# Attention with mixed heads and a gated MLP on one core: the sign of the converted weights set as a bit on VectorE instead of multiplied in on GpSimd

## The chip, the cores and the metric

The kernel runs on one core of one Trainium2 chip, as one program. The metric is its time on the device in microseconds, from the first to the last instruction with what lies around it; lower is better. A core has five engines with a queue each, which run side by side and wait for each other by semaphores: TensorE (PE in the profile, PEld its weight loads), VectorE (DVE), ScalarE (ACT), GpSimd (POOL) and SyncE (SP). Here SP does no arithmetic, it issues nearly all the DMAs. An engine takes its instructions strictly in order: one that waits holds up everything behind it in the same queue. All tensors lie in SBUF while they are worked on; matmuls write to PSUM.

## The reference

```python
# attention: 4 batches, 12 heads, 448 positions, head size 64 (q, k, v, w_pre, w_post)
scores = scale * np.matmul(q, k.transpose(0, 1, 3, 2))
scores = np.einsum('bhij,hg->bgij', scores, w_pre)
scores = scores - np.max(scores, axis=-1, keepdims=True)
attn = np.exp(scores)
attn = attn / (np.sum(attn, axis=-1, keepdims=True) + 1e-09)
attn = np.einsum('bhij,hg->bgij', attn, w_post)
attn_out = np.matmul(attn, v)
x = attn_out.transpose(0, 2, 1, 3).reshape(1792, 768)
# gated MLP, d_model 768, d_ff 1536
g = x @ w_gate
silu = g * (1.0 / (1.0 + np.exp(-g)))
out = (silu * (x @ w_val)) @ w_out
```

The three weight matrices of the MLP come as 64-bit floats. [...]

## The kernel before

The attention runs first, over four batches with 45 row blocks each (reshuffle by DMA, split into a high and a low part, three pre matmuls, max, exp, post matmuls, and per head the product with v); its result goes to HBM as x in a high and a low part. Behind it the MLP runs over two halves of the tokens (first and second batch of 896). For each it goes over 12 blocks f of d_ff: `up` computes g and v for two halves of 448 tokens, with a weight tile of 768 columns per block for each of g and v (a unit; unit 2f is g's, unit 2f + 1 is v's), and three matmuls per product (high times high, low times high, high times low). `gate`, `gated` and `gated_low` make of them the tiles sg, m, gh and gl. Then come three thirds of the output with 4 units each (`down`, `finish`).

In the first half each of the 36 units is loaded as raw 64-bit words (`load_raw`, issued by SP, line 437), converted (`convert`), stored as 32-bit floats for the second half (`keep`, SP, line 475) and split (`split_w`: whi on ACT at line 492, wlo on DVE at line 488). In the second half it is only loaded again (`load_w`) and split. Of raw and mag there are two buffers each, so unit n + 2 can be loaded only when every reader of raw of unit n is done; of w there are three, of whi and wlo four.

`convert` has nine steps, and each is a single instruction. ACT takes the high word, read as a 32-bit float, and makes its magnitude (Abs, line 456) and its sign (Sign, line 458, values 1 and -1). The magnitude is clamped (line 460). DVE works on the integer words: it moves the exponent (462), takes the exponent alone into w (464), shifts the magnitude into place (466), multiplies the low word by it (468) and adds the two (470). The last step multiplies w by the sign (472). `eng`, which clamps and multiplies, is POOL, and DVE for the first three units (EARLY), which are converted while the attention still runs.

The order of the work is written out by numbers: every step is put down with a due time by `at` or, for the MLP, `at_ff`, and `run` sorts by it and issues in that order; the queue of an engine is the sorted list cut to that engine. In the MLP a step of `convert` is due some 16 to 6 units of time ahead of the matmuls that need the weights. There x in `at_ff(n - x, ...)` is read from a list of nine numbers, one per step. Around it the queue of DVE goes round in a fixed turn for each f, two units per turn: m and gl of the two halves lie between the steps of the one unit, and the steps of the other stand together; wlo of a unit stands behind the add (470) of the unit after it.

Of the kernel before, what the change touches and what calls it, by code (L numbers as in the profile page):

```python
# [11 lines left out]
F32 = mybir.dt.float32  # L12
F32R = mybir.dt.float32r
U32 = mybir.dt.uint32
AF = mybir.ActivationFunctionType
ALU = mybir.AluOpType
# [3 lines left out]
def f32_of(bits):  # L20
    return struct.unpack("<f", struct.pack("<I", bits))[0]
# [3 lines left out]
def talking_heads_moe_kernel(ctx, tc, q, k, v, w_pre, w_post, w_gate, w_val, w_out, out):  # L25
    nc = tc.nc
# [3 lines left out]
    P = 128  # L30
# [42 lines left out]
    def at(key, fn):  # L73
        ops.append((key, len(ops), fn))
# [7 lines left out]
    def later(fn, *a):  # L82
        return lambda: fn(*a)
# [43 lines left out]
    def first(c):  # L127
        return c * QT
# [222 lines left out]
    for b in range(B):  # L351
# [3 lines left out]
        for p in range(NPAIR):  # L355
            n = n0 - 22 + 1.9 * p if b else (-30.5 + 0.5 * p if p < 2 else -30.5 + p)
# [3 lines left out]
        for c in range(NC):  # L360

            n = n0 + first(c)
            if (b, c) == (0, 0):
                load, ready, step = -61, -31, 1.0
                score = -29.0
            else:
                before = tiles((c - 1) % NC)
                step = before / NPAIR
# [12 lines left out]
        for t in range(NTB):  # L381
            n = n0 + t
# [12 lines left out]
        for c0, m in parts:  # L395
            last = n0 - (-(c0 + m) * CP // TS) - 1
            for p in range(NPAIR):
                n = last + (5 + p * 1.45 if m == 2 else 4.9 + AVS * p if c0 + m == NC else 5 + AVO + AVS * p)
# [6 lines left out]
    pl = {}  # L405
# [6 lines left out]
    W = NKC * P  # L412
    EARLY = 3
    raws, cvs, w32, wsp, xs_, ups, sgs, ms, g_, yps = ({} for _ in range(10))
# [14 lines left out]
    def unit_index(u):  # L429
        if u[0] == "o":  # L430
            return 2 * NFC + u[1] * (NFC * ET // W) + u[2]
        return 2 * u[1] + (u[0] == "v")
# [9 lines left out]
    def convert(u, step):  # L442
        n = unit_index(u)
        eng = nc.vector if n < EARLY else nc.gpsimd
        if step == 0:
            mag, sgn, w = (
                pl["cv_p"].tile([P, W], F32, tag=x, name=f"{x}_{n}", bufs=k) for x, k in (("mag", 2), ("sgn", 2), ("w", 3))
            )
            cvs[u] = mag, sgn
            w32[0, u] = w  # L450
        mag, sgn = cvs[u]
        w = w32[0, u]
        low, high = raws[u][:, :, 0], raws[u].bitcast(F32)[:, :, 1]
        a, b = mag.bitcast(U32), w.bitcast(U32)
        if step == 0:
            nc.scalar.activation(mag, high, AF.Abs)  # L456
        elif step == 1:
            nc.scalar.activation(sgn, high, AF.Sign)
        elif step == 2:
            eng.tensor_scalar(mag, mag, f32_of(0x38000000), f32_of(0x47EFFFFF), op0=ALU.max, op1=ALU.min)  # L460
        elif step == 3:
            nc.vector.tensor_scalar(a, a, 0x08000000, 4, op0=ALU.bitwise_xor, op1=ALU.logical_shift_left)  # L462
        elif step == 4:
            nc.vector.tensor_scalar(b, a, 1, 0x7F800000, op0=ALU.logical_shift_right, op1=ALU.bitwise_and)
        elif step == 5:
            nc.vector.tensor_scalar(a, a, 1, None, op0=ALU.logical_shift_right)
        elif step == 6:
            nc.vector.scalar_tensor_tensor(w, low, 2.0 ** -52, w, op0=ALU.mult, op1=ALU.mult)
        elif step == 7:
            nc.vector.tensor_tensor(w, mag, w, op=ALU.add)  # L470
        else:
            eng.tensor_tensor(w, w, sgn, op=ALU.mult)  # L472

    def keep(u):
        nc.sync.dma_start(out=w_d[unit_index(u)], in_=w32[0, u])
# [94 lines left out]
    def at_ff(n, fn):  # L570
        at(END + n / 1.8, fn)

    for b in range(NT // TB):
# [7 lines left out]
        for f in range(NFC):  # L581
            n = n0 + f * T_F
# [11 lines left out]
        for e in range(3):  # L594
# [4 lines left out]
            if last:  # L599
                for c in range(NTC):  # L600
                    n = n1 + c * NFC * T_D / NTC
# [10 lines left out]
        for n, u in units:  # L612
            if b:
                at_ff(n - 16, later(load_w, b, u))
                at_ff(n - 8, later(split_w, b, u, False))
                at_ff(n - 7, later(split_w, b, u, True))
            elif unit_index(u) < EARLY:
                n = START + SPACE * unit_index(u)
                at(max(START, n - 4.0), later(load_raw, u))
                for step, x in enumerate((0.4, 0.8, 0.5, 0.5, 1.8, 2.5, 2.9, 4.1, 5.1)):  # L620
                    at(n + x + 0.25, later(convert, u, step))
                at(n + 8.4, later(split_w, b, u, False))
                at(n + 10.6, later(split_w, b, u, True))
                at(n + 6.7, later(keep, u))
            else:
                n -= LEAD
                n1 = END + (n - 21.3) / 1.8
                at(min(n1, B * NTB + 2.75) if unit_index(u) == EARLY else n1, later(load_raw, u))
                for step, x in enumerate((16.2, 15, 15.4, 12.6, 12.1, 11.6, 11.1, 10.2, 5.8)):
                    at_ff(n - x, later(convert, u, step))  # L630
                at_ff(n - 3.8, later(split_w, b, u, False))
                at_ff(n - 2.8, later(split_w, b, u, True))
                at_ff(n - 3.9, later(keep, u))
# [43 lines left out]
```

## Time and profile before

| | |
|---|---|
| median of 3 runs (1045.07 to 1048.63) | 1047.21 us |
| the profiled execution | 1048.95 us |
| its span, from first to last instruction | 1047.2 us |
| PE busy | 1020.7 us, 97% |
| PEld busy | 853.2 us, 81% |
| DVE busy | 597.8 us, 57% |
| ACT busy | 514.1 us, 49% |
| POOL busy | 444.0 us, 42% |
| mean granted clock of TensorE | 0.995 |

A share of the span is an average over stages that differ: the attention up to about 500 us, the first half of the MLP up to about 778 us with the conversion in it, then the second half without it. A busy PE is one that has a matmul under way, not one at its peak. A wait is put down to the one that came last. Times of rows are counted from the start of the span. In the names of tiles a number of the buffer is left out: `mag<-raw` is any unit's.

### The profile page before, as it was taken

To read this page: it belongs to the slowest core of one execution; us is meant where nothing else is said; L and a number is where in the kernel's file an instruction comes from. 1 tells how busy PE (TensorE), PEld (TensorE's weight loads), DVE (VectorE), ACT (ScalarE), POOL (GpSimd) and SP (SyncE) were. 2 spreads that over 40 slices of the span, in tenths; PEclk is the share of its full clock that TensorE was granted. 3 is DMA by queue.
4 is the path that set the end of the run, shared out by engine and by line. 5 is a ranking of instruction groups with operands and counts; after the bars stand their busy time and mean duration, and the time that the engine had idled before them with its cause. 6 is when DMAs were issued, how large, how long until landed. Compare 5 with 4: busy or idle time off the path is not lost.

```text
span 1047.2 us, 17964 instructions
## 1 busy us (share of the span) xinstructions
PE 1020.7 (97%) x6660; PEld 853.2 (81%) x6660; DVE 597.8 (57%) x1181; ACT 514.1 (49%) x1103; POOL 444.0 (42%) x439
## 2 busy tenths in 40 slices
PE   6899999999999999999999999999999999999998
PEld 3577777777777777777898888899999999999998
DVE  4566555657466565577499999998923322332110
ACT  2686776768676676786444434443322222222110
POOL 1675555647465555674375666667600000000000
PEclk9999999999999999998999999999999999999999
DMA  6466443844466443668554444448741112112311
GB/s 125 117 160 172 116 126 112 202 132 125 124 160 176 116 127 113 183 199 244 183 166 151 147 169 138 160 155 289 254 167 46 60 47 61 46 61 62 97 50 36
DMA packets 131055, 140.69 MB, mean 134 GB/s; under 512 B 52552, under 2 KB 114012, under 8 KB 130968
## 3 DMA queue, kind: packets, MB, share of 16 engines
q1 hardware_dynamic: 130776, 139.30, 45.3%
q8 instruction: 53, 0.87, 0.4%
q0 software_dynamic: 192, 0.24, 0.1%
q14 instruction: 34, 0.28, 0.1%
HBM read 70.19 MB, written 30.80 MB: 96 GB/s over the span
## 4 chain that ended last, share of the span: by engine, by line
PE 76%; DVE 13%; ACT 3%; issue 3%; DMA 3%; POOL 2%; SPq 0%; POOLq 0%; ACTq 0%; DVEq 0%
PE post L306 14%; PE qk L224 8%; PE av L328 7%; PE dn L547 5%; PE dn L546 5%; PE dn L548 5%; PE pre L271 5%; PE pre L273 3%; PE pre L272 3%; DVE w L470 3%; DVE mag L462 3%; PE upv L508 3%; PE upv L507 3%; PE upg L512 3%; PE upg L508 3%; PE upg L507 3%
## 5 line engine op out<-in xcount | busy, mean ns | idle before, releaser
L265 POOL TENSOR_TENSOR lo<-rs,hi 120x448 fp32r<-120x448 f32 x180 | 206.5, 1148 | 161.0 <-ACT hi L259 157.6
L306 PEld LDWEIGHTS post<-rw,e 120*112 120x112 f32 (+1 forms) x1440 | 169.9, 177 | 32.2 <-issue 9.6
L306 PE MATMUL post<-rw,e 120*112 120x120 f32 (+1 forms) x1440 | 181.7, 270 | 0.3 <-POOL rw L296 0.3
L460 POOL TENSOR_SCALAR mag<-mag 128x768 f32<-128x768 f32 x33 | 103.8, 3145 | 95.9 <-ACT mag L456 94.1
L547 PE MATMUL dn<-wlo,gh 128*128 128x256 f32 x504 | 141.1, 280 | 0.5 <-DVE wlo L488 0.5
L546 PE MATMUL dn<-whi,gh 128*128 128x256 f32 x504 | 141.0, 280 | 0.0
L548 PE MATMUL dn<-whi,gl 128*128 128x256 f32 x504 | 141.0, 280 | 0.0
L280 DVE TENSOR_REDUCE st<-pre 120x1 f32<-120x448 f32 x180 | 111.8, 621 | 39.8 <-PE pre L273 36.9
L315 ACT ACTIVATE attnT<-post 112x480 f32<-112x480 f32 (+3 forms) x192 | 103.5, 546 | 28.4 <-PE post L306 26.3
L287 ACT ACTIVATE e<-pre,st 120x448 f32<-120x448 f32 x180 | 114.0, 633 | 0.5 <-DVE st L280 0.5
L259 ACT ACTIVATE hi<-rs 120x448 fp32r<-120x448 f32 x180 | 103.9, 577 | 17.7 <-DMA rs<-stg 9.6
L508 PE MATMUL upv<-x,wlo 128*128 128x448 f32 x288 | 106.5, 370 | 4.7 <-DVE wlo L488 4.7
L488 DVE TENSOR_TENSOR wlo<-w,whi 128x768 fp32r<-128x768 f32 x72 | 69.1, 961 | 72.2 <-ACT whi L492 70.8
L230 DVE COPY stg<-qk 110x448 f32<-110x448 f32 (+1 forms) x144 | 85.1, 619 | 43.1 <-PE qk L224 42.5
L507 PE MATMUL upg<-x,whi 128*128 128x448 f32 x288 | 105.8, 367 | 0.0
L508 PE MATMUL upg<-x,wlo 128*128 128x448 f32 x288 | 105.6, 367 | 0.0
L507 PE MATMUL upv<-x,whi 128*128 128x448 f32 x288 | 105.6, 367 | 0.0
L224 PE MATMUL qk<-kk,qt 64*110 64x448 f32 (+1 forms) x384 | 100.3, 594 | 4.4 <-DVE stg L230 2.8
L492 ACT ACTIVATE whi<-w 128x768 fp32r<-128x768 f32 x72 | 60.2, 839 | 87.8 <-POOL w L472 57.9
L528 ACT ACTIVATE gh<-m 128x448 fp32r<-128x448 f32 x48 | 27.8, 579 | 137.8 <-DVE m L523 137.8
L547 PEld LDWEIGHTS dn<-wlo,gh 128*128 128x128 f32 x504 | 94.7, 188 | 0.7 <-DVE wlo L488 0.7
L546 PEld LDWEIGHTS dn<-whi,gh 128*128 128x128 f32 x504 | 94.7, 188 | 0.0
(65 smaller groups left out, 1786.7 us busy)
## 6 DMA issues: line engine op xcount, KB each, us to landing
rs<-stg SPq DMA_DIRECT2D x176, 210.0 KB
w_d<-w SPq DMA_DIRECT2D x36, 384.0 KB
w<-w_d SPq DMA_DIRECT2D x36, 384.0 KB
x<-x_d SPq DMA_DIRECT2D x24, 448.0 KB
x_d<-xs SPq DMA_DIRECT2D x42, 224.0 KB
raw<-in_moe_w_gate_dram SPq DMA_DIRECT2D x12, 768.0 KB
raw<-in_moe_w_val_dram SPq DMA_DIRECT2D x12, 768.0 KB
raw<-in_moe_w_out_dram SPq DMA_DIRECT2D x12, 768.0 KB
```

Source lines behind the costliest of these rows:

```text
L224: nc.tensor.matmul(pt[:m], qt[b, c][hs, p, :m], kk[b, p][hs], start=True, stop=True)
L259: nc.scalar.activation(hi[:n], x[:n], AF.Copy)
L265: nc.gpsimd.tensor_tensor(lo[:n], x[:n], hi[:n].bitcast(F32), op=ALU.subtract)
L280: nc.vector.tensor_reduce(st[:n, 0:1], pt[:n], axis=AX.X, op=ALU.max, negate=True)
L287: nc.scalar.activation(e[:n], pt[:n], AF.Exp, bias=st[:n, 0:1], scale=1.0, accum_out=st[:n, 1:2])
L306: nc.tensor.matmul(pt[:, c, :, :m], e[:n, c * CP:(c + 1) * CP], w[:n, :, :m], start=True, stop=True)
L460: eng.tensor_scalar(mag, mag, f32_of(0x38000000), f32_of(0x47EFFFFF), op0=ALU.max, op1=ALU.min)
L507: nc.tensor.matmul(pt, hi[:, c], xh[:, c, ts], start=(c == 0), stop=False)
L508: nc.tensor.matmul(pt, lo[:, c], xh[:, c, ts], start=False, stop=False)
L546: nc.tensor.matmul(pt, gh, hi, start=opens, stop=False)
L547: nc.tensor.matmul(pt, gh, lo, start=False, stop=False)
L548: nc.tensor.matmul(pt, gl, hi, start=False, stop=closes)
```

## The change

Step 1, Sign on ACT, goes, and with it the tile sgn. The other steps move up by one number. The last step is no longer a float product of w and sgn on POOL (on DVE for the first three units) but one scalar_tensor_tensor on DVE for all 36 units: of the high word of raw all bits but the sign bit are masked out, and the result is or-ed into w, both read as 32-bit integers. So raw has a reader at the end of the conversion, and the store of w and whi wait for DVE instead of POOL. In the MLP the due time of the last step goes from 5.8 to 9.3 ahead of the unit.

```diff
@@ -443,33 +443,31 @@
         n = unit_index(u)
         eng = nc.vector if n < EARLY else nc.gpsimd
         if step == 0:
-            mag, sgn, w = (
-                pl["cv_p"].tile([P, W], F32, tag=x, name=f"{x}_{n}", bufs=k) for x, k in (("mag", 2), ("sgn", 2), ("w", 3))
+            mag, w = (
+                pl["cv_p"].tile([P, W], F32, tag=x, name=f"{x}_{n}", bufs=k) for x, k in (("mag", 2), ("w", 3))
             )
-            cvs[u] = mag, sgn
+            cvs[u] = mag
             w32[0, u] = w
-        mag, sgn = cvs[u]
+        mag = cvs[u]
         w = w32[0, u]
         low, high = raws[u][:, :, 0], raws[u].bitcast(F32)[:, :, 1]
         a, b = mag.bitcast(U32), w.bitcast(U32)
         if step == 0:
             nc.scalar.activation(mag, high, AF.Abs)
         elif step == 1:
-            nc.scalar.activation(sgn, high, AF.Sign)
+            eng.tensor_scalar(mag, mag, f32_of(0x38000000), f32_of(0x47EFFFFF), op0=ALU.max, op1=ALU.min)
         elif step == 2:
-            eng.tensor_scalar(mag, mag, f32_of(0x38000000), f32_of(0x47EFFFFF), op0=ALU.max, op1=ALU.min)
+            nc.vector.tensor_scalar(a, a, 0x08000000, 4, op0=ALU.bitwise_xor, op1=ALU.logical_shift_left)
         elif step == 3:
-            nc.vector.tensor_scalar(a, a, 0x08000000, 4, op0=ALU.bitwise_xor, op1=ALU.logical_shift_left)
+            nc.vector.tensor_scalar(b, a, 1, 0x7F800000, op0=ALU.logical_shift_right, op1=ALU.bitwise_and)
         elif step == 4:
-            nc.vector.tensor_scalar(b, a, 1, 0x7F800000, op0=ALU.logical_shift_right, op1=ALU.bitwise_and)
+            nc.vector.tensor_scalar(a, a, 1, None, op0=ALU.logical_shift_right)
         elif step == 5:
-            nc.vector.tensor_scalar(a, a, 1, None, op0=ALU.logical_shift_right)
+            nc.vector.scalar_tensor_tensor(w, low, 2.0 ** -52, w, op0=ALU.mult, op1=ALU.mult)
         elif step == 6:
-            nc.vector.scalar_tensor_tensor(w, low, 2.0 ** -52, w, op0=ALU.mult, op1=ALU.mult)
-        elif step == 7:
             nc.vector.tensor_tensor(w, mag, w, op=ALU.add)
         else:
-            eng.tensor_tensor(w, w, sgn, op=ALU.mult)
+            nc.vector.scalar_tensor_tensor(b, raws[u][:, :, 1], 0x80000000, b, op0=ALU.bitwise_and, op1=ALU.bitwise_or)
 
     def keep(u):
         nc.sync.dma_start(out=w_d[unit_index(u)], in_=w32[0, u])
@@ -617,7 +615,7 @@
             elif unit_index(u) < EARLY:
                 n = START + SPACE * unit_index(u)
                 at(max(START, n - 4.0), later(load_raw, u))
-                for step, x in enumerate((0.4, 0.8, 0.5, 0.5, 1.8, 2.5, 2.9, 4.1, 5.1)):
+                for step, x in enumerate((0.4, 0.5, 0.5, 1.8, 2.5, 2.9, 4.1, 5.1)):
                     at(n + x + 0.25, later(convert, u, step))
                 at(n + 8.4, later(split_w, b, u, False))
                 at(n + 10.6, later(split_w, b, u, True))
@@ -626,7 +624,7 @@
                 n -= LEAD
                 n1 = END + (n - 21.3) / 1.8
                 at(min(n1, B * NTB + 2.75) if unit_index(u) == EARLY else n1, later(load_raw, u))
-                for step, x in enumerate((16.2, 15, 15.4, 12.6, 12.1, 11.6, 11.1, 10.2, 5.8)):
+                for step, x in enumerate((16.2, 15.4, 12.6, 12.1, 11.6, 11.1, 10.2, 9.3)):
                     at_ff(n - x, later(convert, u, step))
                 at_ff(n - 3.8, later(split_w, b, u, False))
                 at_ff(n - 2.8, later(split_w, b, u, True))
```

The lines of the changed kernel behind 456 are one or two lower: the clamp is 458, the exponent 460, the add 468, the new op 470, wlo 486.

On DVE, in the turn of f = 5 of the first half, the rows from the product of unit 13 with the low word to the first step of unit 14 stand before like this (w_13 and raw_13 are unit 13's, wlo_0_12 is the low part of unit 12 in the first half, m_0_5_0 the gated product of f = 5 in its first half of tokens):

```order
L468 SCALAR_TENSOR_TENSOR w_13_6986<-raw_13_6948,w_13_6986 128x768
L470 TENSOR_TENSOR w_13_6986<-mag_13_6984,w_13_6986 128x768
L488 TENSOR_TENSOR wlo_0_12_7041<-w_12_6919,whi_0_12_7040 128x768
L523 TENSOR_TENSOR m_0_5_0_7068<-sg_0_5_0_7007,upv_0_5_0_7013 128x448
L534 TENSOR_TENSOR gl_0_5_7071<-m_0_5_0_7068,gh_0_5_7070 128x448
L462 TENSOR_SCALAR mag_14_7045<-mag_14_7045 128x768
```

And after:

```order
L466 SCALAR_TENSOR_TENSOR w_13_6959<-raw_13_6923,w_13_6959 128x768
L468 TENSOR_TENSOR w_13_6959<-mag_13_6958,w_13_6959 128x768
L486 TENSOR_TENSOR wlo_0_12_7013<-w_12_6894,whi_0_12_7012 128x768
L470 SCALAR_TENSOR_TENSOR w_13_6959<-raw_13_6923,w_13_6959 128x768
L521 TENSOR_TENSOR m_0_5_0_7040<-sg_0_5_0_6981,upv_0_5_0_6986 128x448
L532 TENSOR_TENSOR gl_0_5_7043<-m_0_5_0_7040,gh_0_5_7042 128x448
L460 TENSOR_SCALAR mag_14_7017<-mag_14_7017 128x768
```

The new op of unit 13 (L470 of the changed kernel) stands behind the low part of unit 12 and ahead of m; nothing else moved. The load of raw for unit 15, which waited for the product with the low word, now waits for this op.

On ACT, in the tail of the attention, between Abs of the second unit (mag_1) and the evacuation of a product with v (xs), before:

```order
L456 ACTIVATE mag_1_5807<-raw_1_5637 128x768
L259 ACTIVATE hi_3_36_5811<-rs_3_36_5702 120x448
L315 ACTIVATE attnT_107<-post_3_29_5796 112x48x10
L458 ACTIVATE sgn_1_5808<-raw_1_5637 128x768
L287 ACTIVATE e_3_33_5828,st_3_33_5801<-pre_3_33_5790,st_3_33_5801 120x448
L337 ACTIVATE xs_3_0_5_5839<-av_3_0_5_5830 128x224
```

And after:

```order
L456 ACTIVATE mag_1_5805<-raw_1_5637 128x768
L259 ACTIVATE hi_3_36_5808<-rs_3_36_5700 120x448
L315 ACTIVATE attnT_107<-post_3_29_5794 112x48x10
L287 ACTIVATE e_3_33_5824,st_3_33_5799<-pre_3_33_5788,st_3_33_5799 120x448
L337 ACTIVATE xs_3_0_5_5835<-av_3_0_5_5826 128x224
```

The Sign of unit 1 is gone and e_3_33, an exp of the attention, stands where it stood.

## Rows read from the trace of the kernel before

**Rows 1.** The profile's page: busy time of the engines, and the chain that ended last, shares of the span by engine.

```profile
PE 1020.7 (97%) x6660; PEld 853.2 (81%) x6660; DVE 597.8 (57%) x1181; ACT 514.1 (49%) x1103; POOL 444.0 (42%) x439
...
PE 76%; DVE 13%; ACT 3%; issue 3%; DMA 3%; POOL 2%; SPq 0%; POOLq 0%; ACTq 0%; DVEq 0%
```

**Rows 2.** The table by stretches, three of 20 us. Columns: stretch and its length, then busy time of PE, PEld, DVE, ACT and POOL with the instructions in brackets, granted clock, DMA share, GB/s.

```profile
540.00:560.00 20.00, 20.00 (x99) 18.29 (x98) 18.37 (x21) 9.11 (x13) 12.73 (x7) 1.00 0.52 175
580.00:600.00 20.00, 19.38 (x96) 17.64 (x95) 18.54 (x24) 9.80 (x15) 10.76 (x6) 1.00 0.39 139
700.00:720.00 20.00, 20.00 (x172) 20.00 (x172) 18.14 (x20) 8.49 (x11) 14.55 (x7) 1.00 0.69 223
```

**Rows 3.** Who waited for whom from 520 to 695 us: us in all, times, the longest.

```profile
ACT whi L492 <- POOL w L472: 19.9, 10, 2.2
...
PEld upv L508 <- DVE wlo L488: 8.0, 9, 1.0
```

**Rows 4.** The instructions of DVE in order of time, one turn of the up-projections of the first batch, with the low part (L488) with which the stage's stalls begin to build up ahead of it and the last one that PE waits for behind it. Columns: start, us, what; in square brackets the idle time before it and what ended it.

```profile
523.93 0.94 DVE L488 TENSOR_TENSOR wlo<-w,whi 128x768 fp32r<-128x768 f32 x1
...
586.90 2.20 DVE L462 TENSOR_SCALAR mag<-mag 128x768 uint32<-128x768 uint32 x1 [0.30 <-POOL mag L460]
...
590.20 0.95 DVE L468 SCALAR_TENSOR_TENSOR w<-raw,w 128x768 f32<-128x768 uint32 x1
591.19 1.46 DVE L470 TENSOR_TENSOR w<-mag,w 128x768 f32<-128x768 f32 x1
592.57 0.94 DVE L488 TENSOR_TENSOR wlo<-w,whi 128x768 fp32r<-128x768 f32 x1
593.44 0.61 DVE L523 TENSOR_TENSOR m<-sg,upv 128x448 f32<-128x448 f32 x1
594.70 1.40 DVE L534 TENSOR_TENSOR gl<-m,gh 128x448 fp32r<-128x448 f32 x1 [0.65 <-ACT gh L528]
596.01 0.55 DVE L462 TENSOR_SCALAR mag<-mag 128x768 uint32<-128x768 uint32 x1
...
597.74 0.62 DVE L534 TENSOR_TENSOR gl<-m,gh 128x448 fp32r<-128x448 f32 x1 [0.18 <-ACT gh L528]
...
601.12 0.95 DVE L488 TENSOR_TENSOR wlo<-w,whi 128x768 fp32r<-128x768 f32 x1
...
611.48 0.55 DVE L462 TENSOR_SCALAR mag<-mag 128x768 uint32<-128x768 uint32 x1
...
693.91 0.95 DVE L488 TENSOR_TENSOR wlo<-w,whi 128x768 fp32r<-128x768 f32 x1
```

**Rows 5.** The instructions of PE in the same turn.

```profile
582.02 0.37 PE L507 MATMUL upg<-x,whi 128*128 128x448 f32 x1
...
585.67 0.37 PE L507 MATMUL upv<-x,whi 128*128 128x448 f32 x1
586.65 0.47 PE L508 MATMUL upv<-x,wlo 128*128 128x448 f32 x1 [0.62 <-DVE wlo L488]
```

**Rows 6.** The instructions of POOL: a clamp with DVE at rest, and those of the same turn.

```profile
505.76 2.78 POOL L460 TENSOR_SCALAR mag<-mag 128x768 f32<-128x768 f32 x1 [9.77 <-ACT mag L456]
...
586.83 1.85 POOL L472 TENSOR_TENSOR w<-w,sgn 128x768 f32<-128x768 f32 x1
590.45 3.33 POOL L460 TENSOR_SCALAR mag<-mag 128x768 f32<-128x768 f32 x1 [1.77 <-ACT mag L456]
593.76 1.85 POOL L472 TENSOR_TENSOR w<-w,sgn 128x768 f32<-128x768 f32 x1
```

**Rows 7.** Conversion steps on DVE by line, over the whole span: ns at least, at the median, at most.

```profile
L468 DVE SCALAR_TENSOR_TENSOR w<-raw,w x36: 946/952/1898, 458.1 to 757.1; 128x768 f32<-128x768 uint32 x36
...
L472 DVE TENSOR_TENSOR w<-w,sgn x3: 947/948/1451, 462.1 to 488.3; 128x768 f32<-128x768 f32 x3
```

**Rows 8.** The chain of waits from 440 to 500 us, two pieces of it: start, us, what.

```profile
451.25 0.83 ACT sgn L458
...
463.38 0.82 ACT sgn L458
```

**Rows 9.** The tail of the attention: SP's queue, DVE and PE in order of time, and the row of the table by stretches for 474 to 481.

```profile
461.87 0.79 SPq L437 DMA_DIRECT2D raw<-in_moe_w_gate_dram  x1
462.76 0.82 SPq L252 DMA_DIRECT2D rs<-stg  x1
...
462.12 0.95 DVE L472 TENSOR_TENSOR w<-w,sgn 128x768 f32<-128x768 f32 x1
...
471.97 0.47 PE L271 MATMUL pre<-hi,w_pre_hi 120*120 120x448 f32 x1 [1.53 <-ACT e L287]
...
474.00:481.00 7.00, 6.62 (x38) 5.12 (x40) 5.32 (x12) 4.00 (x10) 4.12 (x5) 0.51 0.93 279
```

**Rows 10.** SP's queue in order of time in the turn shown above, and the Abs on ACT.

```profile
584.31 0.37 SPq L437 DMA_DIRECT2D raw<-in_moe_w_gate_dram  x1
588.71 0.34 SPq L475 DMA_DIRECT2D w_d<-w  x1
591.22 0.37 SPq L437 DMA_DIRECT2D raw<-in_moe_w_val_dram  x1
...
589.47 0.90 ACT L456 ACTIVATE mag<-raw 128x768 f32<-128x768 f32 x1
```

**Rows 11.** DMA traffic from 584 to 594 us in 40 slices of 0.25 us, GB/s.

```profile
GB/s 0 0 0 0 0 61 106 143 258 332 360 373 373 393 365 299 164 16 0 0 0 0 319 406 406 393 49 0 0 0 0 0 0 49 106 160 279 315 340 393
```

## The prediction

> **What bounds the kernel now.** I read the page first [rows 1]: PE is busy 97% of the span, so nearly all the time is PE's and an edit on DVE, ACT and POOL can only give back what PE waits for. The chain that ended last nevertheless has 13% of DVE in it. The table by stretches tells where [rows 2]: PE is full from 540 to 560, is idle 0.62 us from 580 to 600, and is full again from 700 to 720, with a granted clock of 1.00 in all three. The stretch in the middle belongs to the first pass of up-projections. The waits of 520 to 695 us say on whom [rows 3]: on L488, the low part of the weights on DVE, 8.0 us of weight loads over nine times. So some 8 us is about all that this stage can give.
>
> The pattern is a fixed turn of one f, two units [rows 4]. DVE starts the same L462 at 596.01 and 611.48: a turn is 15.47 us. PE alone needs less: a half takes 3.65 us (582.02 to 585.67), four halves 14.60, and then, before 586.65, it waits 0.62 us for L488 [rows 5]. DVE is the bound of this stage, 18.5 of 20 us busy [rows 2], and part of that is not work. L462 takes 2.20 us at 586.90 and 0.55 at 596.01; L534 takes 1.40 at 594.70, though 0.62 at 597.74. Both long ones stand on POOL's sign products L472, which run from 586.83 and from 593.76 for 1.85 us each [rows 6]. L470 takes 1.46 us at 591.19, where two-input ops of its size take 0.95 [rows 4, 7]: it is held about 0.5 us by the beginning of a clamp on POOL (L460 at 590.45).
>
> **The change part by part.** *POOL's product goes* (33 times, 1.85 us). On POOL it was in nobody's way, but on DVE it cost 2.20 - 0.55 = 1.65 us and 1.40 - 0.62 = 0.78 us per turn [rows 4], 2.4 us together. It also stood ahead of whi on ACT, which waited 19.9 us for it over ten times [rows 3].
>
> *ACT's sign goes* (36 times, 0.9 us). In the turn ACT has time to spare, so there nothing. In the tail of the attention two of the three early ones stand on the chain of waits, 0.83 us at 451.25 and 0.82 at 463.38 [rows 8], with PE idle 1.53 us before 471.97 [rows 9].
>
> *DVE's new op comes* (33 more; the three early ones take the place of a product on DVE). No row shows a bitwise op on two tensors. The nearest is L468, also a scalar_tensor_tensor on the strided words of raw: 0.95 us at the median, 1.90 at most; the tensor_tensor whose place it takes on DVE took 0.95 at the median [rows 7]. Since L462, bitwise as well, is as fast as its float neighbours when free (0.55), I take 0.95. Two per turn: 1.9 us, less than the 2.4 that come free. By DVE's work alone the turn would fall to about 15.47 - 2.4 + 1.9 = 14.97 minus some of DVE's own idle (0.3 and 0.65 us), that is close to PE's 14.60.
>
> *What is late next.* The new op reads raw, so raw is released only behind it, and it stands behind the next L488 in DVE's queue. Before, the release was L468: SP issues the next load at 591.22, right behind the L468 that began at 590.20 and took 0.95, and what was issued in the same way at 584.31 is read by ACT (Abs, L456) at 589.47 [rows 4, 10]. Before, a product on POOL and whi stood in between, so the load was hidden. Now a ring closes over one turn: load, Abs, clamp, chain, low part, sign, release, load. Its terms, for the unit whose L462 stands between L534 and the second L523:
> - L462 to the L488 behind it: 596.01 to 601.12, 5.11 us, with L470's 0.5 us hold in it [rows 4]. The hold stays: whi, Abs and clamp follow gh as before.
> - from L488 to the next op 0.87 (592.57 to 593.44), the new op 0.95, release to issue 0.07 (591.15 to 591.22) [rows 4, 10].
> - the load. Issued at 584.31, its bytes are through in the slice that begins at 588.00, 4.0 us later [rows 11]; Abs reads it at 589.47 with no wait put to the DMA, so it takes at most 5.16 [rows 10]. The report comes behind the last bytes; I take 4.5 as an estimate between the two, nearer to the bytes.
> - Abs begun to clamp begun 589.47 to 590.45, 0.98; the clamp undisturbed 2.78 (505.76), and 0.05 to hand over [rows 6, 10].
>
> Together 5.11 + 0.87 + 0.95 + 0.07 + 4.5 + 0.98 + 2.83 = 15.31 us against 15.47: the ring, not DVE's work, sets the turn. Between the L488 at 523.93, with which the stall begins to build up, and the one at 693.91, on which PE waits last, lie 11 turns [rows 4]; PE runs without a gap behind that. The gain is 11 x 0.16 = 1.8 us. With the load at its lower end the turn is 14.81 and the gain 7.3; at its upper end 15.97 and the loss 5.5.
>
> In the second half of the turn the ring isn't closed: that load is issued behind the other new op and has about 1 us to spare before ACT comes to it behind the second gh. In the down-projections the ring covers two units, and PE takes 20.00 of 20 us there [rows 2]; I count nothing.
>
> *The tail of the attention.* The two signs on the chain could give 1.65 us. Against it: SP issues the third raw load at 461.87, behind L468 of the first unit, and an rs load at 462.76 behind it [rows 9]. The release is now the new op, in the place of the product that DVE began at 462.12, so it comes at 463.07, and the load and the rs loads behind it in SP's queue some 1.3 us later, in a stretch where the DMA is 0.93 busy a little later [rows 9] and hi, which feeds the pre matmuls, waits for rs if it is late. I take the sum as nothing, between -1.65 and +1.3.
>
> SBUF's port between DVE and POOL deserves a sentence, since the new op has two SBUF inputs. L488 ran 0.94 us in the middle of a clamp (592.57, clamp from 590.45 to 593.78), and L470 was held for 0.5 us only [rows 4, 6]. The Trainium skill (SBUF — State Buffer, "SBUF: two separate sides") says that the pair of ports is locked for a whole instruction and the other side fully blocks. L462 under the product agrees (held until it ended), L488 under the clamp doesn't; by that rule L470 would be held some 2 us longer and the turn would be near 17.4, 21 us more in all, which the row of 1.46 excludes.
>
> **The rivals.** *A, the stage becomes PE's.* The load lands in 4.0 us, or the hold of L470 falls beside something else: the turn goes to 14.6 to 14.8 and the gain to between 4 and the 8 us that PE waited, 1039.2 to 1043.2. For it: the slices of the load [rows 11]. Against: the clamp keeps its distance to L468.
>
> *B, slower: the ring is longer than the old turn.* Its place is the raw load. Before, the store of the weight came 4.4 us behind the load (584.31, 588.71) and had the DMA for itself; now both are released by the same op and the store is issued right behind the load. If 384 KB share with 768 KB at the 375 GB/s of the slices [rows 10, 11], the load lands up to 1.0 us later. Each 0.1 us costs 11 x 0.1 = 1.1; from a load of 4.66 on the kernel is slower, at 5.4 by 8 us, 1055. Nothing here shows the two so close together.
>
> *C, ACT's gain comes through.* If the rs loads are in time, 1.65 us are added to the 1.8. Also PE ran at a granted clock of 0.51 from 474 to 481, the lower of its two levels, after the idle time before 471.97 [rows 9]; at the full one these 7 us would take 3.5 less. With both 1040.2, with the first alone 1043.7.
>
> *D, the change doesn't take the sign off the path:* the new op waits for the port like L468 at its 1.90 us [rows 7]. It stands where no clamp runs, so I give it no chance of its own; it would be +0.95 per turn, a part of B's side.
>
> **How the numbers follow.** The profiled execution took 1048.95 us with a span of 1047.20, 1.7 above the median of the runs, 1047.21; the sum is made against the profiled one (1048.95 - 1.8 = 1047.15), and against the median it gives 1047.21 - 1.8 = 1045.4. A measurement of this kernel tells some 0.3%, 3.1 us, from no change. Forecast, a turn between 15.2 and 15.5: 0.50, all within 0.3%. A: 0.20 and C: 0.10, faster. B beyond 3.1 us: 0.15, slower. What is left, 0.05, is small errors of both signs, the same. So faster 0.30, same 0.55, slower 0.15. The range from 1039.5 to 1051 takes in A and C but for their ends, the upper bound of the load in part, and leaves out the far side of B.
>
> **What would show it.** Right: L462 and L534 at 0.55 and 0.62 everywhere in the turn; the new op near 0.95; a wait of 1 to 1.5 us on the L462 between L534 and L523, put to POOL's clamp, which in turn waited for Abs and Abs for raw; PE still waiting for L488 once per turn, 15.2 to 15.4 us apart. Wrong: a turn of 14.6 (A), raw landing over 4.7 us after its issue (B), the half clock at 474 gone (C), or the new op at over 1.2 us.

## The result, and the profile after

The changed kernel is slower: 1060.38 us, median of 4 runs (1059.65 to 1062.89), against 1046.61 us, median of 4 (1045.07 to 1048.63). The ratio is 1.0135, with a 95% interval from 1.0110 to 1.0159: 13.8 us more. The profiled execution took 1059.65 us with a span of 1057.8.

The page first: the busy time of the engines, and the chain that ended last by engine.

```profile
PE 1020.0 (96%) x6660; PEld 855.9 (81%) x6660; DVE 581.4 (55%) x1214; ACT 484.6 (46%) x1067; POOL 373.4 (35%) x406
...
PE 69%; issue 10%; POOL 6%; DMA 4%; ACT 3%; DVE 3%; SPq 0%; POOLq 0%; ACTq 0%; DVEq 0%
```

DVE, ACT and POOL all work less than before [rows 1], PE as much, and the span is 10.6 us longer. So the time went into waiting. In the chain DVE's 13% have shrunk to 3%, POOL has grown from 2% to 6%, and issue, time in which the engine waited for nothing that the profile shows, from 3% to 10%. DMA has hardly moved, from 3% to 4%: the chain doesn't name the load of the ring that is found below, it books the stretch in which that load runs as issue (7.82 us from 604.64).

The table by stretches says where; the first, second and fourth row answer to [rows 2].

```profile
540.00:560.00 20.00, 20.00 (x98) 17.97 (x98) 17.35 (x25) 6.59 (x10) 6.38 (x3) 1.00 0.44 134
580.00:600.00 20.00, 19.01 (x94) 17.30 (x93) 14.25 (x21) 5.32 (x8) 7.59 (x3) 1.00 0.54 174
600.00:620.00 20.00, 17.32 (x78) 15.61 (x78) 17.17 (x24) 7.74 (x12) 7.15 (x3) 0.91 0.38 120
700.00:720.00 20.00, 19.25 (x164) 19.25 (x165) 16.02 (x22) 4.27 (x5) 6.56 (x3) 1.00 0.51 148
720.00:740.00 20.00, 16.99 (x123) 16.78 (x122) 13.56 (x18) 5.02 (x7) 5.54 (x2) 0.83 0.83 270
```

DVE has time to spare now (14.25 us from 580 to 600, where it had 18.54), and PE stands still all the same. In the down-projections it does 123 matmuls from 720 to 740; the row of before for the same 20 us has 173:

```profile
720.00:740.00 20.00, 20.00 (x173) 20.00 (x172) 16.80 (x17) 5.26 (x7) 14.20 (x6) 1.00 0.83 291
```

Who waited for whom from 520 to 695 us, in answer to [rows 3]:

```profile
ACT mag L456 <- DMA raw<-in_moe_w_gate_dram: 38.3, 9, 5.9
...
DVE mag L460 <- POOL mag L458: 16.5, 11, 1.5
...
ACT whi L490 <- DVE w L470: 11.4, 8, 2.9
PEld upv L506 <- DVE wlo L486: 11.4, 8, 3.1
```

The first row had no counterpart before: Abs now waits for the raw load, nine times. What PE's weight loads wait for the low part has risen from 8.0 to 11.4 us. One turn on DVE, to be laid beside [rows 4]:

```profile
599.39 0.56 DVE L460 TENSOR_SCALAR mag<-mag 128x768 uint32<-128x768 uint32 x1 [1.50 <-POOL mag L458]
...
603.13 1.46 DVE L468 TENSOR_TENSOR w<-mag,w 128x768 f32<-128x768 f32 x1
604.51 0.95 DVE L486 TENSOR_TENSOR wlo<-w,whi 128x768 fp32r<-128x768 f32 x1
605.38 0.94 DVE L470 SCALAR_TENSOR_TENSOR w<-raw,w 128x768 uint32<-128x768 uint32 x1
606.25 0.55 DVE L460 TENSOR_SCALAR mag<-mag 128x768 uint32<-128x768 uint32 x1
...
615.30 0.56 DVE L460 TENSOR_SCALAR mag<-mag 128x768 uint32<-128x768 uint32 x1 [1.50 <-POOL mag L458]
```

And what runs between the new op at 605.38 and the L460 at 615.30, on SP, ACT and POOL, in answer to [rows 6, 10]:

```profile
606.39 0.37 SPq L437 DMA_DIRECT2D raw<-in_moe_w_gate_dram  x1
606.81 0.53 SPq L473 DMA_DIRECT2D w_d<-w  x1
...
611.51 0.91 ACT L456 ACTIVATE mag<-raw 128x768 f32<-128x768 f32 x1 [4.31 <-DMA raw<-in_moe_w_gate_dram]
...
612.50 2.77 POOL L458 TENSOR_SCALAR mag<-mag 128x768 f32<-128x768 f32 x1 [6.78 <-ACT mag L456]
```

This is the ring, with every term to be read off: from L460 to the low part 5.12 us (599.39 to 604.51), to the new op 0.87, the op 0.94, to the issue of the load 0.07, the load up to Abs 5.12 (606.39 to 611.51), Abs to clamp 0.99, clamp and handing over 2.80. Together 15.91 us, the turn from 599.39 to 615.30; before it was 15.47. The store of w is issued 0.42 us behind the load. By the semaphore events of the trace a load of this stage landed 4.43 us after its issue before (median), and 5.05 now.

In the down-projections PE stalls three times, the longest at unit 29. DVE there, then SP, then PE:

```profile
725.16 0.56 DVE L460 TENSOR_SCALAR mag<-mag 128x768 uint32<-128x768 uint32 x1 [2.41 <-POOL mag L458]
728.80 0.42 DVE L553 COPY o<-dn 128x256 f32<-128x256 f32 x1 [3.08 <-DMA out_dram<-o]
729.14 1.08 DVE L462 TENSOR_SCALAR w<-mag 128x768 uint32<-128x768 uint32 x1
...
732.60 0.95 DVE L486 TENSOR_TENSOR wlo<-w,whi 128x768 fp32r<-128x768 f32 x1
```

```profile
721.68 0.38 SPq L437 DMA_DIRECT2D raw<-in_moe_w_out_dram  x1
722.83 0.90 SPq L557 DMA_DIRECT2D out_dram<-o  x2
```

```profile
730.19 0.28 PE L546 MATMUL dn<-whi,gl 128*128 128x256 f32 x1
733.60 0.58 PE L545 MATMUL dn<-wlo,gh 128*128 128x256 f32 x1 [3.01 <-DVE wlo L486]
733.98 0.41 PE L546 MATMUL dn<-whi,gl 128*128 128x256 f32 x1
```

And the row of the table by stretches for the 7 us from 732:

```profile
732.00:739.00 7.00, 5.40 (x25) 5.40 (x26) 6.90 (x10) 0.84 (x1) 0.00 (x0) 0.54 0.70 211
```

The fourth copy of a third (L553) takes the buffer of the first, so it waits until that one's store has been read out, and the conversion of the next unit stands behind it in DVE's queue. The store was issued 1.15 us behind a raw load. The low part that PE needs comes at 732.60, PE stands for 3.01 us, and behind that the granted clock is 0.54 over 7 us, the lower of its two levels for most of them: a matmul takes 0.41 us instead of 0.28. Both together cost about 5.9 us: the 3.01, and half of the 5.8 that PE works at the half clock, from 733.6 to 739.4.

The stages of this kernel and of all that follow, in us, from the first matmul of one stage in the trace to that of the next (the attention from the start of the span):

| kernel | attention | up, first batch | down, first batch | up, second batch |
|---|---|---|---|---|
| before | 494.4 | 192.2 | 89.6 | 178.6 |
| changed | 494.1 | 197.9 | 98.2 | 175.1 |
| e1 three raw | 494.9 | 186.9 | 88.7 | 175.1 |
| e2 store by ACT | 494.5 | 192.1 | 96.4 | 178.6 |
| e3 sign early | 492.2 | 194.9 | 93.2 | 178.6 |
| e4 sign ahead | 494.3 | 190.1 | 92.2 | 175.1 |
| e5 four o | 496.5 | 199.4 | 92.3 | 175.1 |
| e6 = e3 + e2 | 492.8 | 194.2 | 95.0 | 175.1 |
| e7 = e1, load held | 490.3 | 185.3 | 88.7 | 175.1 |
| e8 before, three raw | 494.1 | 206.5 | 93.0 | 178.6 |
| e9 before, store moved | 498.1 | 191.9 | 90.5 | 175.1 |
| e10 = e2 + e5 | 493.8 | 195.6 | 92.7 | 178.6 |
| e11 = e10 + e4 | 497.1 | 189.5 | 90.2 | 175.1 |

The changed kernel lost 5.7 us in the first up-projections and 8.7 in the down-projections behind them. The two middle columns answer to the change. The first and the last differ among these traces in a way that no edit explains (last section); by them the single profile shows 10.6 us of loss where the runs show 13.8.

Not all of the 5.7 us is the steady ring. From the low part at 523.59 to the one at 699.75 (L486) the changed kernel takes 176.2 us for the 11 turns, the kernel before 170.0 [rows 4]. Ten of the 11 turns take 15.7 to 15.9 us and one 17.54 (586.97 to 604.51), because one load came 1.7 us later than the others (last section). Without that load the 11 turns would have lost some 4.5 us.

### The profile page after: what moved, and what is told of

Its sections match the earlier page's. It is cut to its first block, busy times and chain, and to the rows that moved or that the text cites. A ratio compares the mean times of both kernels' runs of the same rounds, so it can differ in the third digit from the quotient of the medians.

```text
span 1057.8 us, 17884 instructions
## 1 busy us (share of the span) xinstructions
PE 1020.0 (96%) x6660; PEld 855.9 (81%) x6660; DVE 581.4 (55%) x1214; ACT 484.6 (46%) x1067; POOL 373.4 (35%) x406
## 4 chain that ended last, share of the span: by engine, by line
PE 69%; issue 10%; POOL 6%; DMA 4%; ACT 3%; DVE 3%; SPq 0%; POOLq 0%; ACTq 0%; DVEq 0%
PE post L306 13%; PE qk L224 7%; PE av L328 7%; POOL mag L458 6%; PE pre L271 5%; PE dn L545 4%; PE dn L546 4%; PE dn L544 4%; PE pre L273 3%; PE pre L272 3%; PE upv L505 3%; PE upv L510 3%; PE upv L506 3%; PE upg L506 3%; PE upg L505 3%
## 5 line engine op out<-in xcount | busy, mean ns | idle before, releaser
L458 POOL TENSOR_SCALAR mag<-mag 128x768 f32<-128x768 f32 x33 | 95.7, 2901 | 174.9 <-ACT mag L456 170.3
L486 DVE TENSOR_TENSOR wlo<-w,whi 128x768 fp32r<-128x768 f32 x72 | 69.6, 968 | 71.8 <-ACT whi L490 70.3
L546 PEld LDWEIGHTS dn<-whi,gl 128*128 128x128 f32 x504 | 96.0, 191 | 0.0
```

The source lines that it names most:

```text
L546: nc.tensor.matmul(pt, gl, hi, start=False, stop=closes)
```

## The experiments

Ratios are against the kernel before on the same chip, with 95% intervals. Its median was 1048.43 us beside e1 to e4, 1046.32 beside e5 to e8 and 1048.47 beside e9 to e11.

**e1, three buffers of raw**

```diff
-    for name, bufs in (("raw", 2), ("cv_p", 2), ("ws_p", 4)):
+    for name, bufs in (("raw", 3), ("cv_p", 2), ("ws_p", 4)):
```

> The changed kernel with three buffers of raw instead of two (the room of the former sgn). Theory 1, the ring over the late release of raw: the load of a unit no longer waits for the new op two units back but three, so the ring has one more unit of slack and is open; the turn falls from 15.9 to between PE's 14.6 and 15.0, and the two stalls in the down-projections go as well: 1038 to 1043 us. Theory 2, the time is lost by DVE's own work (two more ops of 0.95 us per turn) or by a port: nothing in the buffers changes that, the turn stays at 15.7 to 15.9, 1056 to 1061 us.

1039.79 us, ratio 0.9912 (0.9881 to 0.9943). PE waits for no low part any more, neither in the up- nor in the down-projections, and it is full in the stretches where it stood:

```profile
580.00:600.00 20.00, 20.00 (x101) 18.53 (x100) 18.83 (x26) 8.00 (x12) 8.77 (x3) 1.00 0.48 154
...
720.00:740.00 20.00, 20.00 (x172) 20.00 (x172) 15.02 (x19) 4.95 (x6) 9.06 (x3) 1.00 0.81 306
```

DVE does the same ops as in the changed kernel and fits into PE's time with them, 18.83 of 20 us. So its work wasn't what made the changed kernel slow: the release of raw was. Theory 1 holds.

**e2, the store issued by ACT**

```diff
-        nc.sync.dma_start(out=w_d[unit_index(u)], in_=w32[0, u])
+        eng = nc.sync if unit_index(u) < EARLY else nc.scalar
+        eng.dma_start(out=w_d[unit_index(u)], in_=w32[0, u])
...
-                at_ff(n - 3.9, later(keep, u))
+                at_ff(n - 2.5, later(keep, u))
```

> The changed kernel with the store of w (for all units but the three early ones) issued by ACT behind the Abs of the unit whose raw load it collided with, instead of by SP 0.42 us behind that load. The late release stays, DVE's work stays. Theory 1a, the store that rides behind the load makes the load 0.55 us longer and so closes the ring: the load lands after 4.4 to 4.5 us again, the turn is 15.2 to 15.4, and the kernel stands near the one before, 1043 to 1050 us with what the down-projections keep of their stalls. Theory 1b, the later release alone is too much: the turn stays over 15.7, 1055 to 1061. Theory 2, DVE's work: the turn stays at 15.9.

1055.68 us, ratio 1.0066 (1.0041 to 1.0090). In the up-projections it is as theory 1a has it: 192.1 us, what the kernel before took. The load there, on SP and at ACT:

```profile
634.19 0.37 SPq L437 DMA_DIRECT2D raw<-in_moe_w_gate_dram  x1
...
638.73 0.92 ACT L456 ACTIVATE mag<-raw 128x768 f32<-128x768 f32 x1 [3.72 <-DMA raw<-in_moe_w_gate_dram]
```

It is in after 4.54 us instead of 5.12. Some other loads of e2 were later: its 11 turns take from 15.08 to 16.13 us, with a median of 15.34. So the ring is as short as theory 1a says, and that the stage's total meets that of before to 0.1 us is luck. But the down-projections kept 6.9 of their 8.7 us, so the total missed what I expected by 6 us: the store of w is not the cause there.

**e3, the sign or-ed in early**

```diff
-            nc.vector.tensor_scalar(a, a, 1, None, op0=ALU.logical_shift_right)
+            nc.vector.scalar_tensor_tensor(b, raws[u][:, :, 1], 0x80000000, b, op0=ALU.bitwise_and, op1=ALU.bitwise_or)
         elif step == 5:
-            nc.vector.scalar_tensor_tensor(w, low, 2.0 ** -52, w, op0=ALU.mult, op1=ALU.mult)
+            nc.vector.scalar_tensor_tensor(a, a, 1, b, op0=ALU.logical_shift_right, op1=ALU.bitwise_or)
         elif step == 6:
-            nc.vector.tensor_tensor(w, mag, w, op=ALU.add)
+            nc.vector.scalar_tensor_tensor(w, low, 2.0 ** -52, w, op0=ALU.mult, op1=ALU.mult)
         else:
-            nc.vector.scalar_tensor_tensor(b, raws[u][:, :, 1], 0x80000000, b, op0=ALU.bitwise_and, op1=ALU.bitwise_or)
+            nc.vector.tensor_tensor(w, mag, w, op=ALU.add)
...
```

> The changed kernel with the new op moved ahead of the product with the low word: the sign is or-ed into the exponent alone, the shift of the magnitude becomes a scalar_tensor_tensor that or-s sign and exponent in, so product and sum come out with their sign. DVE has more work than in the changed kernel (a tensor_scalar of 0.55 becomes a scalar_tensor_tensor of about 0.95, 0.8 us per turn), but raw is released by the product as before the change, about 3 us earlier. Theory 1, the ring: open, turn 14.7 to 15.3, no stalls in the down-projections, 1039 to 1047 us. Theory 2, DVE's work: turn 15.9 plus part of 0.8, 1060 to 1068 us.

1050.09 us, ratio 1.0023 (1.0000 to 1.0046), between the two theories. The clamp no longer holds DVE up (no wait of L460 in the up-projections), so the ring is open. But with 0.8 us more per turn DVE itself is the bound: its turn is 15.56 us (L460 at 579.19 and 594.75) with 0.65 us of idle time in it. So DVE's work has a limit near, which the changed kernel stays under and this one doesn't.

**e4, the new op ahead of the low part**

```diff
-                for step, x in enumerate((16.2, 15.4, 12.6, 12.1, 11.6, 11.1, 10.2, 9.3)):
+                for step, x in enumerate((16.2, 15.4, 12.6, 12.1, 11.6, 11.1, 10.2, 9.9)):
```

> The changed kernel with the new op one place earlier on DVE: ahead of the low part of the unit before (L486) instead of behind it. The same work on DVE, raw released 0.87 us earlier, the low part 0.95 us later. Theory 1, the ring: shorter by 0.87, turn 15.0 to 15.1, some 9 us less over the up-projections, 1046 to 1052 us. Theory 2, DVE's work or a port: the turn stays at 15.9 and the kernel at 1058 to 1062.

1049.35 us, ratio 1.0014 (0.9997 to 1.0030). As the ring has it: turns of 15.07 to 15.28 us, 7.8 us less than the changed kernel in the up-projections (a part of that is the late load of the changed kernel's trace) and 6.0 less in the down-projections, for one place in DVE's queue and no work less.

**e5, four buffers of o**

```diff
-    for name, bufs in (("g_p", NFC), ("t_p", 2), ("o_p", 3)):
+    for name, bufs in (("g_p", NFC), ("t_p", 2), ("o_p", 4)):
```

> The changed kernel with four buffers of the output tile o instead of three. In the down-projections of the changed kernel the fourth copy of a third (DVE, L553) waits up to 4.7 us for the first output store, which now has a raw load just ahead of it, and the conversion chain of a unit stands behind that copy in DVE's queue. Theory D1, this wait is what makes the two stalls of PE (5.9 us at unit 29, 2.4 at unit 33): it goes, and with it 4 to 8 us, 1052 to 1057 us. Theory D2, the ring over the late release of raw makes them, among out stores and x loads that lengthen the load itself: the copy's wait is gone but the stalls stay nearly whole, 1058 to 1062 us. The up-projections stay as they are (turn 15.9) in both.

1055.88 us, ratio 1.0086 (1.0056 to 1.0116). D1 for the larger part: the same place on DVE, where the copy waits for nothing now:

```profile
728.90 0.56 DVE L460 TENSOR_SCALAR mag<-mag 128x768 uint32<-128x768 uint32 x1 [2.26 <-POOL mag L458]
729.38 0.42 DVE L553 COPY o<-dn 128x256 f32<-128x256 f32 x1
729.71 0.55 DVE L462 TENSOR_SCALAR w<-mag 128x768 uint32<-128x768 uint32 x1
```

The down-projections lose 2.8 us instead of 8.7, so 5.9 hung on this wait. The up-projections took 1.5 us more than in the changed kernel, which this edit can't explain; the first f alone took 2.0 more, with a stretch at the half clock in it (514 to 518).

**e6, e3 and e2 together**

> The changed kernel with the sign or-ed into the exponent ahead of the product (raw released by the product, as before the change) and with the store of w issued by ACT, away from the raw load: both terms of the ring at their old size, at 0.8 us more work of DVE per turn. If the ring explains the down-projections as well (D2), they take no more than in the kernel before, within 1.5 us, and the whole is 1045 to 1050 us (DVE's work costs up to 1 us in the up-projections, as in the run without the store's move). If the work of DVE itself is too much there, the 3 to 4 us that the run without the store's move lost stay: 1050 to 1053 us.

1051.66 us, ratio 1.0060 (1.0038 to 1.0083): against what I expected of the ring, 5.5 us are still lost in the down-projections. The total lies in the range of the second case, in which DVE's work is too much there. Raw is released early in this kernel, so the late release is not the only thing that uses up their reserve. The copy waits here too, once 3.07 us, with DVE's longer chain behind it. On the load e6 agrees with e2: by the semaphore events its loads land after 4.44 us (median), those of e3, which differs from it only in who issues the store and when, after 5.01.

**e7, e1 with the load of unit 5 held back**

```diff
-                n1 = END + (n - 21.3) / 1.8
+                n1 = END + (n - 21.3) / 1.8 + (2.4 if unit_index(u) == 5 else 0.0)
```

> The changed kernel with three buffers of raw, and the load of unit 5 held back on SP until behind the last stores of x. In the run with three buffers that load moved ahead of two stores of x; PE then waited 1.67 us for xs before an av matmul at 511, a stretch of 3.4 us at the half clock followed, and the first f took 26.4 us instead of 24.7. If the early load did it, the first f falls back to about 24.7 and the kernel to 1036 to 1039 us; if not, it stays at 1039 to 1042.

1037.46 us, ratio 0.9930 (0.9910 to 0.9951); from e1, measured on another chip, its ratio can't be told apart. The first f fell from 26.4 to 24.8 us as expected. But e5 and e10 had the long first f without an early load, so that this load made it long is not shown. What e1, e5 and e10 share is a stretch of 3.4 us at the half clock there (from 512, 514 and 511 us), which e7 doesn't have.

**e8, a control: the kernel before with three buffers of raw**

```diff
-                pl["cv_p"].tile([P, W], F32, tag=x, name=f"{x}_{n}", bufs=k) for x, k in (("mag", 2), ("sgn", 2), ("w", 3))
+                pl["cv_p"].tile([P, W], F32, tag=x, name=f"{x}_{n}", bufs=k) for x, k in (("mag", 2), ("w", 3))
...
+            sgn = pl["cv_p"].tile([P, W], mybir.dt.bfloat16, tag="sgn", name=f"sgn_{n}", bufs=1)
...
-    for name, bufs in (("raw", 2), ("cv_p", 2), ("ws_p", 4)):
+    for name, bufs in (("raw", 3), ("cv_p", 2), ("ws_p", 4)):
...
-                for step, x in enumerate((16.2, 15, 15.4, 12.6, 12.1, 11.6, 11.1, 10.2, 5.8)):
+                for step, x in enumerate((16.2, 12.4, 15.4, 12.6, 12.1, 11.6, 11.1, 10.2, 5.8)):
```

> A control: the kernel before the change (product by the sign on POOL) with three buffers of raw; to make room sgn is a 16-bit float with one buffer, and Sign is due a little later (12.4 instead of 15). If the gain of the run with three buffers came from the buffer alone, this kernel gains as much: 1036 to 1042 us. By theory 1 the load was hidden before, and DVE's work with the holds by POOL's product sets the turn: it stays at 15.4 to 15.6, 1044 to 1050 us.

1063.29 us, ratio 1.0169 (1.0136 to 1.0202). The control failed: the single sgn makes a wait of its own, Sign on ACT for POOL's product, 37.1 us over twelve times in the up-projections. It says nothing on the buffer. That the kernel before has no use for one in the up-projections is seen only in its waits: no Abs waits for raw there.

**e9, the kernel before with the store put behind a load**

```diff
-                at_ff(n - 3.9, later(keep, u))
+                at_ff(n - 0.6, later(keep, u))
```

> The kernel before the change, with the store of w only moved: it stands on SP directly behind the raw load three units on, so that it is issued some 0.4 us behind a load, as in the changed kernel, while raw is released as before and the product stays on POOL. If the store lengthens the load, raw lands 5.0 to 5.1 us after its issue instead of 4.4 here too; the time stays at 1045 to 1049 us, because before the change ACT comes to the Abs only 5.16 us after the issue. If the longer load came from something else in the changed kernel, it lands at 4.4.

1047.00 us, ratio 0.9996 (0.9974 to 1.0017): no change of the time. The store is issued 0.48 us behind the load (594.99 and 595.47), and by the trace's semaphore events the twelve loads from 563.89 to 649.59 land between 5.00 and 5.24 us after their issue, where 4.43 was the median before. The DMA traffic from 594.5 to 604.5 us in slices of 0.25 us, GB/s, beside [rows 11]:

```profile
GB/s 0 0 0 0 33 0 106 115 164 180 193 180 213 217 270 254 340 389 406 414 430 418 295 135 0 0 0 0 0 0 0 0 0 0 0 0 0 0 8 131
```

One block of load and store in place of two apart, through about 5.5 us behind the issue. So the store right behind makes the load longer, by itself 0.6 us; and before the change that cost nothing, since the load was hidden.

**e10, e2 and e5 together**

> The changed kernel with both moves: the store of w issued by ACT (up-projections back at the turn of before) and four buffers of o (no wait of the copy in the down-projections). What is left is the late release alone. By the sum of the single runs: 0 in the up-projections, about 2.5 us lost in the down-projections, 1047 to 1051 us. If store and copy weren't two separate causes, the down-projections lose 5 us or more, 1052 or over.

1049.42 us, ratio 1.0004 (0.9976 to 1.0031), as the sum of the two has it. The profiled run is its longest (1054.81 us): the up-projections took 3.4 us more than before in it, 1.7 of them in the first f, and late loads made three turns 16.4 to 17.2 us long; the down-projections lose 3.2.

**e11, e10 and e4 together**

> As the run before, and the new op one place earlier on DVE, ahead of the low part: the ring is 0.87 us shorter in both phases, with two buffers of raw still. By the ring the turn comes to PE's 14.6 or 14.7, and the down-projections have a reserve of 0.4 us per unit again: 1041 to 1046 us. If the ring isn't what is left, it stays at 1047 to 1051.

1043.64 us, ratio 0.9961 (0.9938 to 0.9985). With two buffers of raw and all of DVE's work the change now gains, because its ring is shorter: 2.8 us in the up-projections, and the down-projections are within 0.6 us of before.

## Why the prediction was wrong

*What came true.* DVE's terms did: L460 takes 0.56 us behind the clamp, the new op 0.95, and L468 keeps its hold at 1.46. (The sign "L534 at 0.62 everywhere" came half true: of the two in a turn, L532 now, one still takes 0.89, at 612.92, just behind the start of the clamp at 612.50.) The ring closed at the place that the prediction names, and its terms came out at 5.12, 0.87, 0.94, 0.07, 0.99 and 2.80 us against 5.11, 0.87, 0.95, 0.07, 0.98 and 2.83. The wait on L460 is 1.50 us and put to POOL's clamp, which waited for Abs, which waited for raw. The tail of the attention moved by 0.3 us, taken as nothing. Port: L486 ran 0.95 us, from 604.51, inside this clamp:

```profile
602.72 3.00 POOL L458 TENSOR_SCALAR mag<-mag 128x768 f32<-128x768 f32 x1 [3.36 <-ACT mag L456]
```

So the trace again differs from the Trainium skill (SBUF — State Buffer, "SBUF: two separate sides"), by which a pair of ports is locked for a whole instruction.

*The first step that failed: the load, "I take 4.5".* It was 5.12 us up to Abs. I took a value between bounds of a load that had the DMA for itself, though the same sum had the store issued right behind it, and left the longer load to rival B with 0.15. The rows couldn't size it (nothing there showed the two so close), but that they would be close was certain, B's lower end, 4.66, lay only 0.16 above my value, and 5.12 lies within the bounds that the sum itself gave, 4.0 to 5.16. By the prediction's own prices 5.12 costs 11 x (5.12 - 4.66) = 5.1 us; the trace shows some 4.5 without the one late load and 5.7 with it. e2 and e9 show the cause from both sides: without the store behind it the load is back at 4.54 and the stage at 192.1 us; with the store behind it in the kernel before, it lands at 5.0. e3 and e6 show it once more (5.01 and 4.44).

*The second: the down-projections, "I count nothing".* 8.7 us, the larger part, and no rival had it. I read PE's 20.00 of 20 us as proof that the ring had room there. A full engine says that nothing is late, not by how much it is early. A row of before that I passed over tells it, on DVE:

```profile
752.91 0.95 DVE L488 TENSOR_TENSOR wlo<-w,whi 128x768 fp32r<-128x768 f32 x1
```

This low part is unit 33's and is done at 753.86; PE's first matmul of that unit starts at 754.03 in the same trace, the first that reads the low part at 754.15. The reserve was 0.2 to 0.3 us there. It wasn't that small everywhere: at unit 29, where the changed kernel stalls longest, it was 1.2 us (723.39 to 724.59). After the change the ring of two units takes 14.8 us (raw loads issued at 701.62 and 716.40, two units apart), just what PE takes for two (7.39 each, the 88.7 us of e1 over 12 units), where DVE gained nearly 0.5 us per unit before (L488 at 700.83, 707.75 and 714.67, 6.92 apart). So a late copy couldn't be made up for. What made it late is a raw load right ahead of the output stores. Before, the first store of a third was issued 2.81 and 2.37 us behind a raw load (716.14 behind 713.33, 745.71 behind 743.34), and the fourth copy waited 0.42 and 1.00 us; in the changed kernel it is 1.15 and 0.43 us behind (757.71 behind 757.28), and the copy waits 3.08 and 4.71. These two loads were issued within 0.1 us of the end of a new op (720.65 and 756.27, 0.95 and 0.94 long), so here it was the late release that put them there. The copy stands in DVE's queue ahead of a conversion. e5 puts 5.9 us to that wait. The late release isn't the only way to put a load there: in e6, with its early release, a store comes 0.63 us behind a load (748.37 behind 747.74), and that copy waits 3.07 us. The 2.8 that are left I put down to the missing reserve: one buffer more (e1) gives them back whole, a ring 0.87 us shorter with the store moved and four o (e11) but for 0.6. How they are split between the late release and longer loads among the x loads is open: e6 lost 5.5 us with an early release.

*The rivals.* B is what happened, by its mechanism and near its price, in the up-projections; the larger loss, in the down-projections, is none of its. A came only with e1 and e7, where PE is the bound. C didn't come: the half clock near 474 was shorter (3.4 us instead of 6.8 in the trace), but the attention ended no earlier than the spread between traces. D is out: none of the 36 new ops took over 0.954 us.

## What to carry to other kernels

When a change makes a buffer free later, write down the ring that this closes, and ask of each transfer in it what the same release sends off beside it. Where the next stage looks full, read its reserve, from when an operand is done to when it is used, before counting nothing. Room that a change frees (here sgn) may be worth more as one more buffer than the work it saves: the same edit was 1.35% slower with two buffers of raw and 0.9% faster with three. What a third buffer gives without the edit is not shown (e8).

## What the runs showed of the hardware

The up-projections of the second batch, where PE waits for nothing, take either 178.6 or 175.1 us in these thirteen traces, five times the one and eight times the other, and no kernel's edit sorts them. PE's row of the same 20 us, before and after:

```profile
880.00:900.00 20.00, 20.00 (x98) 18.17 (x97) 5.66 (x8) 5.07 (x9) 0.00 (x0) 1.00 0.19 60
```

```profile
880.00:900.00 20.00, 20.00 (x101) 18.53 (x100) 5.37 (x7) 5.01 (x9) 0.00 (x0) 1.00 0.14 43
```

101 matmuls instead of 98, at a granted clock of 1.00 in both. What sets the pace is open. There is one trace of each kernel, so whether a kernel keeps its pace is not shown; that the runs lose 13.8 us, near the profile's 10.6 and these 3.5 together, would fit a pace that changes from execution to execution. It is 3.5 us between two profiles of equal work, so single profiles are compared stage by stage, and totals by the runs. The attention varies as well, from 490.3 to 498.1 us.

One raw load of the changed kernel's up-projections was much later than the others there. It was issued at 588.85, and Abs read it 6.75 us later:

```profile
595.60 0.91 ACT L456 ACTIVATE mag<-raw 128x768 f32<-128x768 f32 x1 [5.93 <-DMA raw<-in_moe_w_gate_dram]
```

PE then waited 2.68 us for the low part, until 605.51, and from 606 to 610 the granted clock was 0.57, the lower of its two levels for most of that time. Why the load was late is open.
